# Splitting the first four token loads of a fused transformer block over two issuing engines

## Chip, cores and metric

The kernel runs on one core of a Trainium2 chip. The metric is device time in microseconds for one execution of the whole block, the median of several runs. The profile is of one further execution.

## What is computed

A pre-norm block over 2048 tokens of width 640 with 32 heads of 20: layer norm, query, key and value projections, attention in four segments of 512 tokens with a compressive memory carried from segment to segment, output projection and residual; then a second layer norm, a two-layer feed-forward net of width 1728 with SiLU, and a residual.

```python
x = A_x
h = x + _A_ref(_layernorm(x), A_wq, A_wk, A_wv, A_wo, A_beta)   # attention with memory, 4 segments
h2 = h + _B_ref(_layernorm(h), B_w1, B_w2)                      # silu(x @ w1) @ w2
...
# _A_ref, per segment s:
logits = jnp.einsum('bhqd,bhkd->bhqk', qs, ks) * scale + mask
p = _softmax(logits, axis=-1)
a_dot = jnp.einsum('bhqk,bhkd->bhqd', p, vs)
...
o = g * a_mem + (1.0 - g) * a_dot
M = M + jnp.einsum('bhld,bhle->bhde', phi(ks), vs)
```

All inputs and the output are bf16.

## The kernel before

The tokens are 16 blocks of 128. Segment s holds the blocks 4s to 4s+3. Each segment has a front (layer norm, transposes, projections), ticks (scores, exponentials and weighted sums, one head group of four at a time), a memory update and a back (output projection, second layer norm, feed-forward). Work of neighbouring segments overlaps.

Everything is declared as tasks with the tiles that they read and write. The order of the tasks is a written list, `ORDER` (line 362): every engine carries out its own tasks in the order of that list, and one tracker derives the semaphore waits from the tiles. A name such as `x1:1` means task x1 with buffer 1; a suffix such as `/S` or `/A` chooses the engine where a task allows several. An engine never overtakes: an instruction that waits holds up all behind it on the same engine.

The list begins with these rows:

```python
halfc:0 mt2 mta2 x0:0 mt3 iota sel mt1 zpad x1:1 x2:2 vpad0 mta3 n1_st0:0 epsc x3:3 mt0 warm:0 n1_rs0 w_q:0 n1_st1:6
n1_rs1 n1_st2:2 n1_rs2 n1_st3:3 n1_rs3 n1_ap1:0 mtb3 re_wq2/G:0 w_k fill20:0 fill9:0 re_wk3/G:0 n1_tp1:2 n1_te1/A:1 n1_ap0:1
```

The tasks around the change are these.

- x0 to x3 (line 579) load the token blocks 0 to 3 into `x_tok`, 160 KB each, one transfer a block. w_q, w_k and w_wv (line 582) load the query, key and value weights, 800 KB each, the first two into space that is later `sT`. beta (line 591) loads the 32 gates, repeated over the partitions. All are issued by SyncE (SP) in the order of the list: x0, x1, x2, x3, wq, wk, wv, beta. The later loads, of which the second token group (blocks 4 to 7) and then wo come first, wait until the first fifth of the key weights is repacked.
- n1_st (lines 721 and 724, VectorE) takes the statistics of a block, two halves and their aggregate; n1_rs (lines 730 and 732, GpSimd) adds epsilon and raises to the power -0.5; n1_ap (line 738, VectorE) normalises into a buffer of `xn_rot`. VectorE's order is the statistics of the blocks 0, 1, 2, 3 and then the normalisation of the blocks 1, 0, 2, 3. Block 1 and block 3 share buffer 0 of `xn_rot`, so the normalisation of block 3 waits until block 1 has been transposed.
- n1_tp (line 747, TensorE) transposes a block by five matmuls against an identity, in the order 1, 0, 2, 3; n1_te (lines 756 on ScalarE and 757 on VectorE) writes the result to `tT`, the blocks 1, 0 and 3 on ScalarE and block 2 on VectorE.
- re_wq and re_wk (lines 694 and 696; VectorE, ScalarE and GpSimd) repack the query and key weights by head into `wqr` and `wkr`, in five parts each.
- pr (lines 546 and 547, TensorE) are the projections, qe (lines 831 and 832) their evictions. The first projection needs all four blocks in `tT` and one part of `wqr`.
- fill20 and fill9 (line 616, TensorE) are 29 matmuls of the zero tile `zpad`, which stand in TensorE's order ahead of the first transpose. warm (line 597, ScalarE) is one activation on the same tile, ahead of all other work of ScalarE, with the load of the function table before it. ScalarE issues no transfer in this kernel.

The lines that declare the loads:

```python
def dma(name, reads, writes, fn, prio, bw, kind="plain", lane=None, engs=(SP,)):
    ln = T.lane(name) if lane is None else lane
    ...
def load_x(b0, n, prio, bw=2.1, kind="plain", engs=(SP, AC)):
    s0 = b0 % 12
    dma(f"x{b0}", [(W["wk"], [0])] if b0 >= 4 else [], [(X[b], [0]) for b in range(b0, b0 + n)],
        lambda e: e.dma_start(out=x_tok[:, s0:s0 + n, :], in_=xv[:, b0:b0 + n, :]), prio, bw, kind, engs=engs)
```

A lane is a semaphore of its own, so each load can be waited for by itself. Where `engs` holds one engine and the list names none, the task goes to that one.

Of the kernel before, what the change touches and what calls it, by code (L numbers as in the profile page):

```python
# [11 lines left out]
PE, AC, DV, PO, SP = "pe", "act", "dve", "pool", "sp"  # L12
# [453 lines left out]
def build(nc, es, A_x, A_wq, A_wk, A_wv, A_wo, A_beta, B_x, B_w1, B_w2, out):  # L466
# [89 lines left out]
    def dma(name, reads, writes, fn, prio, bw, kind="plain", lane=None, engs=(SP,)):  # L556
        ln = T.lane(name) if lane is None else lane

        def emit(eng):
            T.add(eng, lambda e: fn(e), reads=R(*reads), writes=R(*writes), lane=ln)  # L560
        cost = {"tr": 1.31, "plain": 0.47, "sb": 0.72, "fix": 0.47}[kind]
        t = G.task(name, {e: cost for e in engs}, emit, reads, writes, prio, mode=kind, bw=bw)
        return t
# [12 lines left out]
# [5 lines that stand above are left out]
    def load_w(k, dst, src, prio, bw, wr, kind="plain", engs=(SP, AC)):  # L581
        dma("w_" + k, [(W["wk"], [0])] if kind == "plain" else [], wr, lambda e: e.dma_start(out=dst, in_=src), prio, bw, kind, engs=engs)

    cw = lambda w: w.rearrange("(c p) e -> p c e", p=128)
    load_x(0, 1, -100, 2.30, "fix", (SP,))
    load_x(1, 1, -99, 2.33, "fix", (SP,))
    load_w("wv", wv_sb[:, :, :], cw(A_wv), -98, 4.96, [(W["wv"], [0])], "fix", (SP,))
    load_x(2, 1, -97, 4.79, "fix", (SP,))
    load_x(3, 1, -96, 4.82, "fix", (SP,))
    dma("beta", [], [(C, ["beta_bc"])],  # L590
        lambda e: e.dma_start(out=beta_bc[:, :],
                              in_=A_beta.rearrange("(o n) -> o n", o=1).to_broadcast([128, H])), -92, 4.65, "fix")
# [642 lines left out]
def bass_sequential_preLN__memory_aug_infini_attn__dense_activation_silu__prompt_kernel(  # L1235
    nc, A_x, A_wq, A_wk, A_wv, A_wo, A_beta, B_x, B_w1, B_w2, out
):
    es = ExitStack()
    with es:
        T, finals, _ = build(nc, es, A_x, A_wq, A_wk, A_wv, A_wo, A_beta, B_x, B_w1, B_w2, out)  # L1240
        with nc.Block() as block:
            T.emit(nc, block, es, final_waits=finals)
# [28 lines left out]
```

## Time and profile before

| | |
|---|---|
| median of 3 runs | 300.82 us (300.63 to 301.13) |
| profiled execution | 301.27 us |
| its span, first to last instruction | 299.5 us |
| TensorE, matmuls | 281.5 us busy, 94% |
| VectorE | 223.3 us, 75% |
| ScalarE | 211.5 us, 71% |
| GpSimd | 146.5 us, 49% |
| transfers | 24.79 MB, mean 83 GB/s |
| granted TensorE clock | full in every slice |

The span is shorter than the execution's time by what lies before its first and after its last instruction. Matmuls are pipelined, so TensorE's busy share isn't its share of peak. SPq is the issuing of transfers by SyncE: its rows show how long an issue takes, not the transfer; the time to landing is counted from the start of the issue to the last of the semaphore's updates. DVE is VectorE, ACT ScalarE, POOL GpSimd, PE TensorE and PEld its weight loads.

### The profile page before, as it was taken

What the parts mean: (1) busy time and instruction counts of PE and PEld (TensorE: products, weight loads), DVE (VectorE), ACT (ScalarE), POOL (GpSimd) and SP (SyncE); (2) the same over time, 40 slices, a digit from 0 to 9 for tenths busy, and PEclk for the clock granted to TensorE, in tenths of its full rate; (3) what the DMA queues carried; (4) which work ended last, traced back from release to release, by engine and by line L of the source; (5) the groups of instructions that cost most, each with busy time, mean ns of one, the idle gap of its engine ahead of it and who ended that gap; (6) DMA issues with size and microseconds to landing.
All of it is one profiled execution on the core that took longest, in us unless ns stands there. A gap on an engine that the chain in (4) does not pass through costs nothing.

```text
span 299.5 us, 9583 instructions
## 1 busy us (share of the span) xinstructions
PE 281.5 (94%) x4069; PEld 158.7 (53%) x4096; DVE 223.3 (75%) x455; ACT 211.5 (71%) x271; POOL 146.5 (49%) x294
## 2 busy tenths in 40 slices
PE   6899789979979999998999999999999999999996
PEld 4553345536634444565654554666654556764574
DVE  6699999788997777779878967497764875727622
ACT  3598999999889999965789858868888651004500
POOL 5767487664945735634743852555854420300000
PEclk9999999999999999999999999999999999999999
DMA  7766937965644410164438521601130032333001
GB/s 208 258 187 141 163 50 174 180 144 103 120 91 37 134 21 2 24 85 92 81 93 126 48 44 24 96 14 33 22 66 2 2 40 51 81 74 109 3 22 66
DMA packets 48586, 24.79 MB, mean 83 GB/s; under 512 B 38880, under 2 KB 47456, under 8 KB 48544
## 3 DMA queue, kind: packets, MB, share of 16 engines
q1 hardware_dynamic: 48544, 24.19, 39.0%
q8 instruction: 32, 0.52, 0.7%
q14 instruction: 10, 0.08, 0.1%
HBM read 10.41 MB, written 2.62 MB: 44 GB/s over the span
## 4 chain that ended last, share of the span: by engine, by line
PE 72%; DVE 11%; ACT 9%; DMA 4%; issue 2%; SPq 1%; POOL 0%; ACTq 0%; DVEq 0%; POOLq 0%
PE ps_all L546 38%; PE ps_all L547 17%; ACT PT L914 8%; PE ps_all L901 6%; PE ps_all L949 4%; PE ps_all L616 2%; PE ps_all L978 2%; DMA tT<-otok 1%; DMA tT<-xn_rot 1%; DMA phiKt<-phiK 1%; PE ps_all L982 1%; DVE on L1015 1%; DVE QK L832 1%; DVE phiQ L851 1%; DVE xn_rot L738 1%
## 5 line engine op out<-in xcount | busy, mean ns | idle before, releaser
L914 ACT ACTIVATE PT<-ps_all 128x1024 bf16<-128x1024 f32 x160 | 154.8, 1027 | 22.3 <-PE ps_all L901 21.3
L926 POOL TENSOR_SCALAR_AFFINE_SELECT PT<-PT 128x512 bf16<-128x512 bf16 x128 | 81.9, 646 | 59.6 <-ACT PT L914 56.2
L1160 ACT ACTIVATE th<-ps_all 128x512 f32<-128x512 f32 (+1 forms) x56 | 31.7, 586 | 32.5 <-PE ps_all L546 25.7
L546 PE MATMUL ps_all<-w_sb,sT 128*128 128x320 bf16 x360 | 52.1, 300 | 0.0
L1166 DVE SCALAR_TENSOR_TENSOR sT<-th,ps_all 128x512 bf16<-128x512 f32 (+1 forms) x56 | 36.3, 663 | 20.5 <-ACT th L1160 20.1
L546 PEld LDWEIGHTS ps_all<-w_sb,sT 128*128 128x128 bf16 x360 | 34.3, 98 | 14.8 <-issue 1.5
L546 PE MATMUL ps_all<-tT,w_sb 128*128 128x512 bf16 x161 | 37.5, 379 | 1.0 <-DVE sT L1166 0.3
L721 DVE BATCH_NORM_STATS2 stt<-x_tok 128x6 f32<-128x320 bf16 x64 | 27.8, 476 | 1.1 <-DMA x_tok<-in_A_x_dram 1.0
L1023 POOL TENSOR_TENSOR otok<-on 128x320 bf16<-128x320 bf16 x24 | 19.4, 812 | 15.4 <-DVE on L1015 12.3
L546 PEld LDWEIGHTS ps_all<-tT,w_sb 128*128 128x128 bf16 x172 | 15.9, 98 | 18.2 <-DVE sT L1166 1.1
L1202 DVE SCALAR_TENSOR_TENSOR x_tok<-ps_all,x_tok 128x640 bf16<-128x640 f32 (+1 forms) x17 | 13.2, 780 | 14.6 <-PE ps_all L546 14.4
L949 PE MATMUL ps_all<-PT,Vx 128*32 128x384 bf16 (+3 forms) x512 | 22.9, 301 | 0.7 <-DVE w_sb L832 0.7
L964 DVE TENSOR_SCALAR oTs<-ps_all,lsc 128x512 bf16<-128x512 f32 x28 | 20.8, 744 | 3.7 <-PE ps_all L949 3.6
L547 PE MATMUL ps_all<-tT,w_sb 128*32 128x512 bf16 x352 | 22.4, 380 | 0.0
L730 POOL TENSOR_TENSOR rst<-mvt,eps_c 128x1 f32<-128x1 f32 x32 | 6.8, 214 | 30.0 <-DVE mvt L724 30.0
L1015 DVE TENSOR_TENSOR on<-ps_all,rd 128x640 bf16<-128x640 f32 x24 | 19.8, 824 | 0.8
L832 DVE CAST QK<-ps_all 128x512 bf16<-128x512 f32 x25 | 17.0, 683 | 4.1 <-PE ps_all L546 2.6
L732 POOL TENSOR_TENSOR rst<-rst,eps_c 128x1 f32<-128x1 f32 x32 | 18.3, 571 | 2.5
L738 DVE TENSOR_SCALAR xn_rot<-x_tok,mvt,rst 128x640 bf16<-128x640 bf16 x32 | 16.6, 534 | 2.9 <-POOL rst L732 1.9
L546 PE MATMUL ps_all<-wv_sb,tT 128*128 128x320 bf16 x120 | 18.3, 300 | 0.3 <-ACT PT L914 0.2
L949 PEld LDWEIGHTS ps_all<-PT,Vx 128*32 128x32 bf16 x512 | 12.0, 96 | 10.8 <-issue 2.6
L901 PE MATMUL ps_all<-QK 20*128 20x512 bf16 (+3 forms) x240 | 15.1, 301 | 2.6 <-DVE QK L832 1.2
(91 smaller groups left out, 389.9 us busy)
## 6 DMA issues: line engine op xcount, KB each, us to landing
out_dram<-x_tok SPq DMA_DIRECT2D x15, 160.0 KB, 1.9
w_sb<-in_B_w_dram SPq DMA_DIRECT2D x5, 432.0 KB, 4.6
x_tok<-in_A_x_dram SPq DMA_DIRECT2D x3, 640.0 KB, 6.1
w_sb<-in_B_w_dram SPq DMA_DIRECT2D x3, 480.0 KB, 5.1
QKV<-QK SPq DMA_DIRECT2D x12, 72.0 KB
sT<-in_A_wq_dram SPq DMA_DIRECT2D x1, 800.0 KB, 6.6
sT<-in_A_wk_dram SPq DMA_DIRECT2D x1, 800.0 KB, 8.3
wv_sb<-in_A_wv_dram SPq DMA_DIRECT2D x1, 800.0 KB, 9.8
```

What stands on the lines that cost most here:

```text
L546: return [lambda e: e.matmul(out, lhsT=lhsT, rhs=rhs, start=start, stop=stop)]
L547: return [lambda e, p=p: e.matmul(out[p:p + 32, :], lhsT=lhsT[:, p:p + 32], rhs=rhs, start=start, stop=stop, tile_position=(0, p)) for p i ...
L721: T.add(DV, lambda e, hh=hh: e.bn_stats(out=stt[:, s, 6 * hh:6 * hh + 6], in_=xb[:, 320 * hh:320 * hh + 320]), reads=R((xa, xsub)), writes ...
L832: (lambda e: e.tensor_copy(out=o, in_=i_))
L901: fns.append(lambda e, j=j, o=o, r=r, q0=q0, q1=q1, qa=qa, ka=ka: e.matmul(ps_all[:, o:o + q1 - q0], lhsT=ka[32 * r:32 * r + DH, 128 * j:1 ...
L914: T.add(AC, lambda e: e.activation(out=pt[:, pta.slot, q0:q0 + 2, 0:width], in_=sc3[:, b0:b0 + 2, 0:width], func=ACT.Exp, scale=SCALE), re ...
L926: fns.append(lambda e, v=v: e.affine_select(out=v, in_=v, pattern=[[0, 4], [1, 128]], compare_op=ALU.is_ge, fill=0.0, base=0, channel_mult ...
L949: fns.append(lambda e, j=j, r=r, h=h, pa=pa, pt=pt, co=co, q0=q0, ji=ji: e.matmul(bank(po)[32 * r:32 * r + 32, q0:hi], lhsT=Vx[:, vx.slot, ...
L964: f = lambda e: e.tensor_scalar(out=o, in0=i_, scalar1=lsc[:, g:g + 1], scalar2=None, op0=ALU.mult)
L1015: T.add(DV, lambda e: e.tensor_tensor(out=on[:, ona.slot, :, :].rearrange("p b (x e) -> p b x e", e=DH), in0=v[:, :, :, 0:DH], in1=r2.unsq ...
L1160: T.add(AC, lambda e: e.activation(out=th[:, tha.slot, lo:hi], in_=bank(ps)[:, lo:hi], func=ACT.Tanh, scale=0.5), reads=R((ps, [0])), writ ...
L1166: T.add(DV, lambda e: e.scalar_tensor_tensor(out=sT[:, f, lo:hi], in0=th[:, tha.slot, lo:hi], scalar=1.0, in1=bank(ps)[:, lo:hi], op0=ALU. ...
```

## The change

x1 and x3 are given to ScalarE. Since the list puts both ahead of warm, they are ScalarE's first two instructions, ahead of its table load. SyncE issues x0, x2, wq, wk, wv, beta. The list is the same, and the orders of TensorE, VectorE and GpSimd stay as they are. The transfers are the same in shape, size and number.

```diff
     load_x(0, 1, -100, 2.30, "fix", (SP,))
-    load_x(1, 1, -99, 2.33, "fix", (SP,))
+    load_x(1, 1, -99, 2.33, "fix", (AC,))
     load_w("wv", wv_sb[:, :, :], cw(A_wv), -98, 4.96, [(W["wv"], [0])], "fix", (SP,))
     load_x(2, 1, -97, 4.79, "fix", (SP,))
-    load_x(3, 1, -96, 4.82, "fix", (SP,))
+    load_x(3, 1, -96, 4.82, "fix", (AC,))
```

The numbers in these calls are hints of a planner that made the list; with the list written out they have no effect.

## The prediction

> **What bounds the kernel now.** I read the page first, then the chain that ended last, the waits and the timeline of the first 25 us, and the single issues of the token loads.
>
> ```profile
> span 299.5 us, 9583 instructions
> PE 281.5 (94%) x4069; PEld 158.7 (53%) x4096; DVE 223.3 (75%) x455; ACT 211.5 (71%) x271; POOL 146.5 (49%) x294
> PE 72%; DVE 11%; ACT 9%; DMA 4%; issue 2%; SPq 1%; POOL 0%; ACTq 0%; DVEq 0%; POOLq 0%
> ```
>
> TensorE is busy 94% of the span and carries 72% of the chain; transfers carry 4%. The change touches only the first issues, so the question is what starts TensorE's real work. The chain answers in order of time (start, duration, what):
>
> ```profile
> 2.66 5.83 PE ps_all L616 x29
> 8.49 0.29 PE ps_all L747 x5
> ...
> 8.81 1.90 ACT tT L756 x3
> ...
> 10.76 4.50 PE ps_all L547 x80
> ...
> 20.65 2.16 PE ps_all L546 x15
> ...
> 22.83 0.83 DVE Vx L799
> ```
>
> The 29 filler matmuls (L616) multiply a zero tile. They start when VectorE has written that tile and run to 8.49 in TensorE's fixed order, ahead of the first transpose (L747). No token block is in this chain before 8.49. Then come five matmuls that transpose block 1, three ScalarE evictions and the first projection at 10.76; TensorE and then VectorE carry on from there without a transfer. So an earlier token block brings nothing unless the fillers were waiting for it, and they do not; a later one costs once it has used up the slack of the layer norm that runs beside the fillers.
>
> The timeline of that layer norm (start, busy, engine, in brackets the idle time before and what ended it):
>
> ```profile
> 3.12 0.89 DVE L721 BATCH_NORM_STATS2 stt<-x_tok 128x6 f32<-128x320 bf16 x2 [0.52 <-DMA x_tok<-in_A_x_dram]
> ...
> 5.41 0.89 DVE L721 BATCH_NORM_STATS2 stt<-x_tok 128x6 f32<-128x320 bf16 x2 [0.17 <-DMA x_tok<-in_A_x_dram]
> ...
> 6.46 0.83 DVE L721 BATCH_NORM_STATS2 stt<-x_tok 128x6 f32<-128x320 bf16 x2
> ...
> 7.45 1.11 DVE L738 TENSOR_SCALAR xn_rot<-x_tok,mvt,rst 128x640 bf16<-128x640 bf16 x3
> ...
> 7.97 0.64 POOL L732 TENSOR_TENSOR rst<-rst,eps_c 128x1 f32<-128x1 f32 x1
> ...
> 8.92 0.45 DVE L738 TENSOR_SCALAR xn_rot<-x_tok,mvt,rst 128x640 bf16<-128x640 bf16 x1 [0.36 <-POOL mt L659]
> ```
>
> VectorE takes the blocks 0, 1, 2, 3. It waits 0.52 us for x0 and 0.17 us for x2; x1 and x3 are there in time. The fourth normalisation, at 8.92, writes buffer 0 of xn_rot, whose last reader is the transpose of block 1. That ends at 8.49 + 0.29 = 8.78, while GpSimd's power for block 3 ends at 7.97 + 0.64 = 8.61. The view names GpSimd's next instruction, but that one isn't needed; by the code it is TensorE's transpose. So GpSimd is 0.17 us early, and the statistics of block 3 may come 0.17 us later for nothing. The three other normalisations are done by 7.45 + 1.11 = 8.56, also ahead of 8.78.
>
> **The change part by part.** The issues of the load queue before:
>
> ```profile
> 0.81 1.83 SPq L579 DMA_DIRECT2D x_tok<-in_A_x_dram  x4
> 2.68 0.43 SPq L582 DMA_DIRECT2D sT<-in_A_wq_dram  x1
> 3.16 0.53 SPq L582 DMA_DIRECT2D sT<-in_A_wk_dram  x1
> 3.73 0.56 SPq L582 DMA_DIRECT2D wv_sb<-in_A_wv_dram  x1
> 4.33 1.60 SPq L591 DMA_DIRECT2D beta_bc<-in_A_beta_dram  x1
> ```
>
> The four token issues run from 0.81 to the next issue at 2.68: 1.87 / 4 = 0.47 us each. Two leave the queue, so x2 is issued at 1.28 and not 1.75, and wq, wk, wv and beta each 2 x 0.47 = 0.94 us earlier (wq at 1.74).
>
> ScalarE gets two issues ahead of its table load:
>
> ```profile
> 0.80 1.28 ACT L597 ACT_TABLE_LOAD   x1 [0.80 <-PEq L1256]
> 2.64 1.27 ACT L597 ACTIVATE w_sb<-zpad 128x1280 bf16<-128x1280 bf16 x1 [0.55 <-DVE zpad L595]
> 8.81 1.90 ACT L756 ACTIVATE tT<-ps_all 128x640 bf16<-128x640 f32 x3 [4.90 <-PE ps_all L747]
> ```
>
> No ScalarE issue is in this trace. By the SP rows both take 0.94 us: x1 goes out at about 0.80 and x3 at 1.27, which is 0.48 and 0.95 us earlier than before, and the table load moves to 1.74. The warm-up activation ends at 2.64 + 1.27 = 3.91 before and by about 4.4 after (1.74 + 1.28 + 1.27 = 4.29). ScalarE then has nothing until 8.81, after 4.90 us of idle time, so this costs nothing; even two issues at the 1.60 us of beta's row would end the warm-up by 6.6.
>
> When the blocks land. One answer for each of the four issues, x0 to x3 (duration of the issue in ns, its start, and the time to landing):
>
> ```profile
> L579 SPq DMA_DIRECT2D x_tok<-in_A_x_dram x1: 408/408/408, 0.8 to 0.8; - x1
> ...
> DMA to landing us min/median/max: 2.3/2.3/2.3
> ```
>
> ```profile
> L579 SPq DMA_DIRECT2D x_tok<-in_A_x_dram x1: 417/417/417, 1.3 to 1.3; - x1
> ...
> DMA to landing us min/median/max: 2.3/2.3/2.3
> ```
>
> ```profile
> L579 SPq DMA_DIRECT2D x_tok<-in_A_x_dram x1: 432/432/432, 1.7 to 1.7; - x1
> ...
> DMA to landing us min/median/max: 3.7/3.7/3.7
> ```
>
> ```profile
> L579 SPq DMA_DIRECT2D x_tok<-in_A_x_dram x1: 432/432/432, 2.2 to 2.2; - x1
> ...
> DMA to landing us min/median/max: 4.0/4.0/4.0
> ```
>
> So x0 lands at 0.8 + 2.3 = 3.1, x1 at 1.28 + 2.3 = 3.6, x2 at 1.7 + 3.7 = 5.4, and x3 at 2.2 + 4.0 = 6.2 for a use at 6.46. After the change x3 goes out 0.95 us sooner and needn't be late. x2 lands no later than its 5.4 unless the whole stream is slower. What can become later is x0, since x1 now goes out beside it instead of 0.47 us behind it. Its tolerance: the 0.17 us for which VectorE waits for x2 vanishes if x2 is in time, and 0.17 us are spare at GpSimd. Together 0.34 us, so x0 may land at 3.44 for nothing. To price a shared start I take the stream's rates by the microsecond (the last column is GB/s; 1 GB/s is 1 KB in a us):
>
> ```profile
> 1.00:2.00 1.00, 0.00 (x0) 0.00 (x0) 0.28 (x1) 1.00 (x1) 0.93 (x7) 1.00 0.17 15
> 2.00:3.00 1.00, 0.34 (x2) 0.28 (x3) 0.60 (x2) 0.45 (x2) 0.71 (x5) 1.00 0.87 287
> 3.00:4.00 1.00, 1.00 (x7) 0.69 (x5) 0.88 (x2) 0.91 (x1) 0.00 (x0) 1.00 1.01 178
> ```
>
> By 3.0 there are 15 + 287 = 302 KB through, and the 320 KB of x0 and x1 by 3.0 + 18/178 = 3.1. If the two share the stream evenly, x0 is through only then instead of at 2.0 + 145/287 = 2.5, 0.6 us later, less what lies between the last bytes and the landing, which was 3.1 - 2.5 = 0.6 us for x0 and 3.6 - 3.1 = 0.5 us for x1. So x0 lands at 3.1 + 0.5 = 3.6, and TensorE's first projection moves by 3.6 - 3.44 = 0.16 us. The lower end is x0 landing at 3.1 as before: 0.00. A gain is excluded here, since the fillers end at 8.49 either way. I take the middle, +0.1 us.
>
> [...] No run here shows two queues yet.
>
> The weights. They land up to 0.94 us earlier. Who waits for them:
>
> ```profile
> POOL wkr L696 <- DMA sT<-in_A_wk_dram: 1.4, 1, 1.4
> ...
> DVE wkr L696 <- DMA sT<-in_A_wk_dram: 1.0, 1, 1.0
> ...
> POOL wqr L696 <- DMA sT<-in_A_wq_dram: 0.5, 1, 0.5
> ```
>
> These waits are real, but behind them VectorE and ScalarE wait again, for TensorE:
>
> ```profile
> 12.50 0.69 DVE L832 CAST w_sb<-ps_all 128x512 bf16<-128x512 f32 x1 [0.27 <-PE ps_all L547]
> ...
> 12.71 2.05 PEld L547 LDWEIGHTS ps_all<-tT,wkr 128*32 128x32 bf16 x40
> ...
> 13.15 0.60 ACT L831 ACTIVATE w_sb<-ps_all 128x512 bf16<-128x512 f32 x1 [0.80 <-PE ps_all L547]
> ```
>
> TensorE is the chain from 10.76 to 22.8 but for short gaps and takes the key weights at 12.71 with no wait. So earlier weights lengthen those waits by what they shorten the first: 0.00. The next loads on SP (the second token group and wo) wait for the key weights' repacking and move earlier too, with nothing behind them that the chain names. If the cover were gone, all 0.94 us could show; that is the lower end.
>
> Sum: 0.00 (ScalarE) + 0.1 (x0) + 0.00 (weights) = +0.1 us. The profiled execution took 301.27 us, 1.8 more than its span; the median of the three runs is 300.82. The same step on the median gives 300.9 us. About 0.2%, 0.6 us, is what a measurement of this kernel can tell from no change.
>
> **The rivals.**
>
> *x0 lands much later.* The stream falls from 287 to 178 GB/s between 3 and 4 us, just after the weights are issued (2.68 to 4.33). If their issuing makes that dip, it moves 0.94 us earlier, onto x0 and x1. Then by 3.0 only 15 + 178 = 193 KB are through, the 320 KB at 3.0 + 127/178 = 3.7, x0 lands at 4.2, and 4.2 - 3.44 = 0.76 us go through the statistics, the normalisations and the transposes to the first projection: 301.6 us. It decides from a landing after 3.44 and shows as slower from 4.04. For it: the dip stands right behind these issues, and x2 and x3, which lie in it, took 3.7 and 4.0 us against 2.3. Against it: x0 and x1 are issued ahead of the weights on their queues, and the trace does not show that the weights' issues cause the dip.
>
> *The earlier weights carry through.* If VectorE's and GpSimd's repacking, 0.94 us ahead, shortens what follows after 22.8, where the chain goes over to VectorE, the time falls by up to 0.94 us: 299.9. Against it: every chain piece from 10.76 to 22.8 is TensorE's.
>
> *The second queue doesn't start when ScalarE does.* If ScalarE's issues land 1 us later than I assume, x1 (needed when x0's statistics are done, at 3.12 + 0.89 = 4.01 at the earliest) and x3 (needed at 6.46) land at 0.80 + 1 + 2.3 = 4.1 and at most 1.27 + 1 + 4.0 = 6.3; the statistics slip by 0.1 us, inside the 0.34 us: 300.8.
>
> **How the numbers follow.** Forecast 0.5, the late queue 0.06: both within 0.2%. x0 much later 0.27. Weights carry through 0.17, which takes in that the first 10 us, with other phases between the engines, come out better for a reason that I don't see. The forecast alone spans 300.5 to 301.3 (the step's two ends and the spread of the three runs, 300.63 to 301.13). The range goes down to 300.0, nearly all of the weights' gain, and up to 301.9, the late x0 at 301.6 and the same spread above it. Faster 0.17, same 0.56, slower 0.27.
>
> **What would show it.** In the profile after: the fillers still 2.66 to 8.49; the first projection at 10.76 to 10.9; x0's first statistics between 3.1 and 3.6 and no wait for x2; two issues on ScalarE ahead of the table load; wq issued near 1.74 and the waits for wk shorter by up to 0.94 us, with the waits of L831 and L832 for TensorE longer. Wrong would be a first projection after 11.3, a filler that starts later, or an equal first projection with another end, which would put the cause behind 10.76.

## The result and the profile after

The changed kernel takes 301.85 us (median of 22 runs, 300.60 to 304.51) against 300.77 us of the kernel before on the same chip (22 runs, 299.15 to 303.14): a ratio of 1.004, 95% interval 1.0025 to 1.0054, which is 0.8 to 1.6 us. The forecast was no change that can be measured, at 300.9 us; it is slower. A few executions of several kernels, at a granted clock of 0.989 to 0.994, are 2 to 4 us longer than the others; such an execution counts in the ratios below where it is less than 1.5% above the fastest of its kernel.

The profiled execution of the changed kernel took 301.62 us with a span of 299.9 us. Outside the span lie 1.7 us, against 1.8 us before, so the loss is inside it. The lines of its page:

```profile
span 299.9 us, 9610 instructions
PE 283.8 (95%) x4096; PEld 158.1 (53%) x4096; DVE 224.1 (75%) x455; ACT 211.3 (70%) x271; POOL 146.7 (49%) x294
q10 hardware_dynamic: 288, 0.33, 0.4%
q14 instruction: 10, 0.08, 0.1%
PE 71%; ACT 14%; DVE 9%; DMA 2%; issue 1%; POOL 1%; SPq 0%; ACTq 0%
```

The queue rows give packets, MB and share. The new queue q10 carries ScalarE's two blocks. ScalarE's share of the chain rises from 9% to 14%. The timeline of the start (start, busy, engine, in brackets the idle time before and what ended it):

```profile
0.80 0.88 ACTq L579 DMA_DIRECT2D x_tok<-in_A_x_dram  x2
0.81 0.90 SPq L579 DMA_DIRECT2D x_tok<-in_A_x_dram  x2
1.72 1.28 ACT L597 ACT_TABLE_LOAD   x1 [1.72 <-PEq L1256]
1.75 0.44 SPq L582 DMA_DIRECT2D sT<-in_A_wq_dram  x1
2.66 4.82 PE L616 MATMUL ps_all<-zpad 128*128 128x256 bf16 x29 [2.66 <-DVE zpad L595]
3.01 1.27 ACT L597 ACTIVATE w_sb<-zpad 128x1280 bf16<-128x1280 bf16 x1
3.87 0.89 DVE L721 BATCH_NORM_STATS2 stt<-x_tok 128x6 f32<-128x320 bf16 x2 [1.27 <-DMA x_tok<-in_A_x_dram]
...
4.92 0.83 DVE L721 BATCH_NORM_STATS2 stt<-x_tok 128x6 f32<-128x320 bf16 x2
...
7.89 2.04 DVE L738 TENSOR_SCALAR xn_rot<-x_tok,mvt,rst 128x640 bf16<-128x640 bf16 x4
...
12.99 0.69 DVE L832 CAST w_sb<-ps_all 128x512 bf16<-128x512 f32 x1 [0.98 <-PE ps_all L547]
...
13.63 0.60 ACT L831 ACTIVATE w_sb<-ps_all 128x512 bf16<-128x512 f32 x1 [1.01 <-PE ps_all L547]
```

Both queues start at 0.8 us. x0, the one block that was needed first, comes 0.75 us later: the first statistics start at 3.87 instead of 3.12. The three blocks behind it are then in time. The fillers, which the prediction had ending at 8.49 "either way", end at 2.66 + 4.82 = 7.48. The chain that ended last up to the first projection (start, duration, what):

```profile
0.81 3.04 DMA x_tok<-in_A_x_dram
...
8.35 0.82 PE ps_all L747 x10
9.17 0.78 DVE xn_rot L738
9.95 0.05 issue
9.99 0.47 PE ps_all L747 x5
10.46 0.02 issue
10.48 0.71 ACT tT L756
11.20 0.04 issue
11.24 1.90 PE ps_all L547 x29
```

x0 lands at 0.81 + 3.04 = 3.85 and now heads the chain, with no filler in it. The fourth normalisation takes 0.78 us where it took 0.45, and the first projection starts at 11.24 instead of 10.76.

That is 0.48 us at the start. A second loss lies far from the edit. ScalarE's timeline at 52 to 56 us and at 160 to 162 us, first of the kernel before, then of the changed one:

```profile
52.66 3.95 ACT L914 ACTIVATE PT<-ps_all 128x1024 bf16<-128x1024 f32 x4
...
160.97 0.60 ACT L1160 ACTIVATE th<-ps_all 128x512 f32<-128x512 f32 x1 [0.16 <-PE ps_all L546]
```

```profile
52.18 2.85 ACT L914 ACTIVATE PT<-ps_all 128x1024 bf16<-128x1024 f32 x3
55.40 1.02 ACT L914 ACTIVATE PT<-ps_all 128x1024 bf16<-128x1024 f32 x1 [0.37 <-PE ps_all L901]
...
161.32 0.60 ACT L1160 ACTIVATE th<-ps_all 128x512 f32<-128x512 f32 x1 [0.43 <-PE ps_all L901]
```

Four exponentials ran back to back before; now there is a hole of 0.37 us ahead of the fourth. At the same place of the feed-forward the idle time goes from 0.16 to 0.43 us. What TensorE makes of the second hole, before and after:

```profile
166.52 0.28 PE L1063 MATMUL ps_all<-Vx,phiKt 128*32 128x42 bf16 x16
166.93 0.40 PE L901 MATMUL ps_all<-QKV 20*128 20x256 bf16 x8
```

```profile
166.59 0.28 PE L1063 MATMUL ps_all<-Vx,phiKt 128*32 128x42 bf16 x16
167.27 0.40 PE L901 MATMUL ps_all<-QKV 20*128 20x256 bf16 x8 [0.40 <-ACT PT L914]
```

The step from one to the other is 0.41 us before and 0.68 us after, so this hole passes to TensorE in full (+0.27). Of the first hole, ScalarE's start is 0.30 us later and 0.18 us are won back at the sixth exponential behind it, which waits 0.18 us less; 0.12 to 0.13 us reach TensorE. Together 0.4 us where they arise.

What is left of all this at the end can be read off TensorE's 4096 weight loads, which have the same order in both kernels, by setting each against its counterpart in the trace of before. The changed kernel's are 0.49 us late at 20 us, 0.56 at 60 us, only 0.07 at 150 us, 0.34 from 169 us on and 0.36 at the end. So in this pair of traces the second hole is most of the difference of the spans (299.9 against 299.5), and the late start is mostly lost again by 150 us.

### The profile page after: what moved, and what is told of

It is laid out like the page before. It is cut to its first block, busy times and chain, and to the rows that moved or that the text cites. A ratio compares the mean times of both kernels' runs of the same rounds, so it can differ in the third digit from the quotient of the medians.

```text
span 299.9 us, 9610 instructions
## 1 busy us (share of the span) xinstructions
PE 283.8 (95%) x4096; PEld 158.1 (53%) x4096; DVE 224.1 (75%) x455; ACT 211.3 (70%) x271; POOL 146.7 (49%) x294
## 4 chain that ended last, share of the span: by engine, by line
PE 71%; ACT 14%; DVE 9%; DMA 2%; issue 1%; POOL 1%; SPq 0%; ACTq 0%
PE ps_all L546 40%; PE ps_all L547 17%; ACT PT L914 12%; PE ps_all L901 6%; PE ps_all L949 4%; PE ps_all L978 2%; DVE stt L721 2%; ACT th L1160 1%; PE ps_all L982 1%; DMA tT<-otok 1%; DMA x_tok<-in_A_x_dram 1%; DVE xn_rot L738 1%; DVE on L1015 1%; DVE QK L832 1%; DVE w_sb L832 1%
## 5 line engine op out<-in xcount | busy, mean ns | idle before, releaser
L546 PE MATMUL ps_all<-tT,w_sb 128*128 128x512 bf16 x172 | 39.8, 379 | 0.4 <-DVE rd L1009 0.3
L832 DVE CAST QK<-ps_all 128x512 bf16<-128x512 f32 x25 | 17.0, 683 | 4.1 <-PE ps_all L546 2.6
```

The lines of the kernel that those rows point to most:

```text
L546: return [lambda e: e.matmul(out, lhsT=lhsT, rhs=rhs, start=start, stop=stop)]
L832: (lambda e: e.tensor_copy(out=o, in_=i_))
```

## The experiments

Each row is one kernel; the ratio is to the kernel before on the same chip, with its 95% interval. "More" is the number of instructions that ScalarE has more than in the kernel before. The two holes are the idle times of ScalarE at the places above; a dash means none shown, or the 0.15 to 0.16 us of the kernel before.

| kernel | ratio | more | holes | fillers end | first statistics | first projection | span |
|---|---|---|---|---|---|---|---|
| before | 1 | 0 | - | 8.49 | 3.12 | 10.76 | 299.5 |
| before, once more | one execution, 300.48 us | 0 | - | 8.07 | 3.11 | 11.13 | 298.8 |
| changed | 1.0040 (1.0025 to 1.0054) | 2 | 0.37, 0.43 | 7.48 | 3.87 | 11.24 | 299.9 |
| changed, once more | 1.0040 (1.0022 to 1.0058) | 2 | 0.38, 0.43 | 7.83 | 3.82 | 11.19 | 300.6 |
| weights held | 1.0051 (1.0029 to 1.0073) | 2 | 0.38, 0.43 | 8.52 | 3.89 | 11.26 | 300.5 |
| x1 later | 1.0114 (1.0071 to 1.0156) | 2 | 0.37, 0.43 | 7.94 | 3.17 | 11.20 | 299.9 |
| both held | 1.0029 (1.0007 to 1.0050) | 2 | 0.38, 0.43 | 8.13 | 3.18 | 10.39 | 299.4 |
| copy held | 1.0042 (1.0014 to 1.0071) | 2 | 0.37, 0.43 | 8.10 | 3.80 | 10.84 | 300.5 |
| before, two activations more | 1.0009 (0.9986 to 1.0031) | 2 | 0.36, 0.43 | 8.55 | 3.18 | 10.81 | 299.4 |
| order swapped | 1.0015 (0.9995 to 1.0036) | 0 | - | 7.41 | 3.61 | 10.64 | 298.8 |
| 24 fillers | 1.0003 (0.9978 to 1.0028) | 0 | - | 7.41 | 3.19 | 10.90 | 299.3 |
| x1 alone | 0.9995 (0.9976 to 1.0014) | 1 | - | 7.42 | 3.92 | 11.20 | 299.3 |
| changed, one activation more | 1.0022 (1.0002 to 1.0043) | 3 | - | 7.86 | 3.86 | 10.89 | 300.6 |
| both held, one activation more | 1.0015 (0.9990 to 1.0041) | 3 | - | 7.71 | 3.05 | 10.75 | 299.4 |

**Why x0 is late: the shared start or the weights.** The first experiment keeps both queues and holds back the query weights, and with them all behind them, until the zero tile is written, so that they are issued as late as in the kernel before. The second keeps the early weights and holds back x1 until a mask is written.

```diff
-            T.add(eng, lambda e: fn(e), reads=R(*reads), writes=R(*writes), lane=ln)
+            T.add(eng, lambda e: fn(e), reads=R(*reads) + (C.keys(["zpad"]) if name == "w_q" else []), writes=R(*writes), lane=ln)
```

> The changed kernel, but SyncE issues the query weights (and all behind them) only when the zero tile is written, at about 2.65 us as before the change instead of 1.75; x1 and x3 stay on ScalarE. Theory A, x0 shares the stream with x1 from its first packets: x0 still lands at 3.6 to 3.9 us, the first statistics start then and the time is 0.7 to 1.2 us over the kernel before. Theory B, the earlier issue of the weights slows the stream under x0: x0 lands by 3.3 us and the time is within 0.3 us of the kernel before.

The second has `C.keys(["mt2"]) if name == "x1"` in that place.

> The changed kernel, but ScalarE issues x1 only after one of GpSimd's first masks, at about 1.5 us instead of 0.80, and x3 behind it; SyncE as in the change, with the weights early. Theory A (shared start): x0 lands at 3.1 to 3.3 us and the time is within 0.3 us of the kernel before, or up to 0.3 us below it since VectorE no longer waits for x2. Theory B (early weights): x0 lands after 3.5 us and the time is 0.7 us or more over the kernel before.

The timeline with the weights held (issue of wq, the first statistics):

```profile
2.63 0.39 SPq L582 DMA_DIRECT2D sT<-in_A_wq_dram  x1
...
3.89 0.89 DVE L721 BATCH_NORM_STATS2 stt<-x_tok 128x6 f32<-128x320 bf16 x2 [1.29 <-DMA x_tok<-in_A_x_dram]
```

wq goes out at 2.63, and x0 is as late as in the changed kernel (3.89 against 3.87). So the weights are not what delays x0. With x1 at 1.42 instead of 0.80, x0 is back:

```profile
3.17 0.89 DVE L721 BATCH_NORM_STATS2 stt<-x_tok 128x6 f32<-128x320 bf16 x2 [0.57 <-DMA x_tok<-in_A_x_dram]
4.45 0.89 DVE L721 BATCH_NORM_STATS2 stt<-x_tok 128x6 f32<-128x320 bf16 x2 [0.15 <-DMA x_tok<-in_A_x_dram]
...
6.81 0.89 DVE L721 BATCH_NORM_STATS2 stt<-x_tok 128x6 f32<-128x320 bf16 x2 [0.24 <-DMA x_tok<-in_A_x_dram]
```

It is the shared start. In this kernel it is x1 and x3 that come late, behind the early weights, and the first projection is as late as in the changed kernel (11.20). Its ratio of 1.0114 rests on six executions, of which four took 301.61 to 302.78 us and two 305.42 and 305.61, so its size means little. But the middle of the four, 302.3, is still 1.7 us over the 300.60 of the kernel before on that chip, more than any step of its trace explains; this stays open.

**Is a late x0 dear in itself? And the fillers?** The kernel before with x1 ahead of x0 in the list, all on SyncE; and the kernel before with 24 fillers instead of 29.

```diff
-halfc:0 mt2 mta2 x0:0 mt3 iota sel mt1 zpad x1:1 x2:2 vpad0 mta3 n1_st0:0 epsc x3:3 mt0 warm:0 n1_rs0 w_q:0 n1_st1:6
+halfc:0 mt2 mta2 x1:1 mt3 iota sel mt1 zpad x0:0 x2:2 vpad0 mta3 n1_st0:0 epsc x3:3 mt0 warm:0 n1_rs0 w_q:0 n1_st1:6
```

> The kernel before, all loads on SyncE, with x1 issued first and x0 second; VectorE still takes x0 first. x0 then lands at 3.5 to 3.6 us instead of 3.1. If the landing of x0 sets the start of TensorE's work in the mean run, the first statistics start at 3.6, 0.45 us late, of which 0.17 us are made up at x2: 0.3 us over the kernel before. If the fillers set it, as the prediction had it: 0.1 us. If the landing of x0 doesn't matter: 0.0.

```diff
-n1_rs1 n1_st2:2 n1_rs2 n1_st3:3 n1_rs3 n1_ap1:0 mtb3 re_wq2/G:0 w_k fill20:0 fill9:0 re_wk3/G:0 n1_tp1:2 n1_te1/A:1 n1_ap0:1
+n1_rs1 n1_st2:2 n1_rs2 n1_st3:3 n1_rs3 n1_ap1:0 mtb3 re_wq2/G:0 w_k fill20:0 fill4:0 re_wk3/G:0 n1_tp1:2 n1_te1/A:1 n1_ap0:1
```

> The kernel before with 24 filler matmuls instead of 29. At 213 ns each they end by 7.8 us at the latest, ahead of the first normalised block at 7.85. If the fillers bind in the mean run, as the prediction had it, the first projection comes up to 0.35 us earlier and the time is 0.3 us lower. If the fillers mostly end before the layer norm, since their spacing falls from 213 to 109 ns at a time that differs from run to run (7.75 us in the profile of before, 5.79 in that of after): within 0.2 us, and the first transpose waits for VectorE.

TensorE's timeline, first with the order swapped (29 fillers), then with 24:

```profile
2.66 4.75 PE L616 MATMUL ps_all<-zpad 128*128 128x256 bf16 x29 [2.66 <-DVE zpad L595]
8.09 1.76 PE L747 MATMUL ps_all<-ident,xn_rot 128*128 128x128 bf16 x20 [0.67 <-DVE xn_rot L738]
10.64 2.34 PE L547 MATMUL ps_all<-tT,wqr 128*32 128x512 bf16 x40 [0.79 <-ACT tT L756]
```

```profile
2.66 4.75 PE L616 MATMUL ps_all<-zpad 128*128 128x256 bf16 x24 [2.66 <-DVE zpad L595]
7.66 1.76 PE L747 MATMUL ps_all<-ident,xn_rot 128*128 128x128 bf16 x20 [0.25 <-DVE xn_rot L738]
10.90 2.34 PE L547 MATMUL ps_all<-tT,wqr 128*32 128x512 bf16 x40 [1.48 <-POOL wqr L696]
```

29 fillers took as long here as 24 there. With the order swapped, x0 is 0.5 us late, the fillers end early, and the first projection is earlier than in the kernel before. With 24 fillers the projection waits for GpSimd's repacking of the query weights. Neither time can be told from the kernel before. So the fillers bind in some executions, as in the trace of before, and not in others.

**The stretched normalisation.** In the changed kernel the fourth normalisation runs beside GpSimd's repacking of the query weights, which begins at 9.24, and takes 0.78 us. This kernel is the changed one with the three GpSimd repackings moved behind that normalisation in the list and the first of them waiting for it. The wait (the edit of the list is left out):

```diff
-                T.run(eng, fns, R(*rr), R(*ww))
+                T.run(eng, fns, R(*rr) + ([("xn", 0, 0)] if (k, c) == ("wq", 2) else []), R(*ww))
```

> The changed kernel, but GpSimd's first copy of the query weights waits until VectorE has normalised block 3. In the profile of the changed kernel that normalisation took 0.79 us beside this copy, and 0.45 us in the profile of before, where the copy had hardly begun. If the copy stretches it: 0.45 us again, the first projection near 10.9 us instead of 11.24, the time 0.3 us under the changed kernel and still 0.4 to 0.8 us over the kernel before. If the stretch has another cause: 0.79 us still, and the time of the changed kernel.

The four normalisations take 1.70 us together instead of 2.04, and the first projection starts at 10.84. So the overlap does stretch it, by 0.34 us. But the time stays where it was, at 1.0042. The next kernel holds back both, x1 until the mask and wq until the zero tile, and the kernel before was profiled once more, unchanged.

```diff
-            T.add(eng, lambda e: fn(e), reads=R(*reads), writes=R(*writes), lane=ln)
+            T.add(eng, lambda e: fn(e), reads=R(*reads) + (C.keys([{"w_q": "zpad", "x1": "mt2"}[name]]) if name in ("w_q", "x1") else []), writes=R(*writes), lane=ln)
```

> Both holds together: ScalarE issues x1 at about 1.4 us and x3 behind it, SyncE the weights at about 2.65 us. Theory (a load issued beside x0 delays x0, and weights issued ahead of x3 delay x3): x0 lands at 3.1 to 3.2 us, x3 by 5.5 us, VectorE waits for no block after x0, the first projection starts at 10.3 to 10.7 us unless the fillers end late, and the time is between 0.3 us under and 0.2 us over the kernel before. If the second queue costs by itself: 0.5 us or more over.

> The kernel before, unchanged, for another draw of the time at which the matmul spacing falls from 213 to 109 ns. If that time is free of the kernel, the 29 fillers end elsewhere than at 8.49 us, and where they end by 7.9 us the first projection starts at 10.3 to 10.6 us, set by VectorE, instead of 10.76. If the 8.49 us is fixed for this kernel: 8.4 to 8.6 again.

TensorE's timeline of the kernel with both held, and the chain of the kernel before in its second trace:

```profile
2.66 5.47 PE L616 MATMUL ps_all<-zpad 128*128 128x256 bf16 x29 [2.66 <-DVE zpad L595]
...
10.39 2.34 PE L547 MATMUL ps_all<-tT,wqr 128*32 128x512 bf16 x40 [0.88 <-ACT tT L756]
```

```profile
2.68 7.33 DMA sT<-in_A_wq_dram
10.01 0.05 issue
10.07 0.93 POOL wqr L696 x2
11.00 0.14 issue
11.13 1.89 PE ps_all L547 x29
```

These two turn the question round. With both held the first projection is the earliest of all, 10.39, and the kernel is still slower than the one before, by 0.2 to 1.5 us where at most 0.2 was expected. The kernel before, in another execution, starts it at 11.13, as late as the changed one, because wq landed at 10.01 instead of 9.26; that execution is among the shortest (298.8 us). The start cannot be the whole cause.

**One issue alone.** The changed kernel with x3 back on SyncE.

```diff
-    load_x(3, 1, -96, 4.82, "fix", (AC,))
+    load_x(3, 1, -96, 4.82, "fix", (SP,))
```

> Half of the change: x1 on ScalarE at 0.80 us, x3 stays on SyncE behind x2, so the weights go out 0.47 us earlier and not 0.94. Theory A (shared start): x0 lands at 3.6 to 3.9 us, the first projection starts near 11.2 us and the time is 0.7 to 1.2 us over the kernel before, all of the change's loss. If the loss needs both loads on ScalarE: x0 lands by 3.4 us and the time is within 0.4 us.

```profile
3.92 0.89 DVE L721 BATCH_NORM_STATS2 stt<-x_tok 128x6 f32<-128x320 bf16 x2 [1.31 <-DMA x_tok<-in_A_x_dram]
```

x0 is as late as in the changed kernel, the first projection is at 11.20, and there is no loss: 0.9995 (0.9976 to 1.0014). So a late x0 alone doesn't cost the 0.7 to 1.2 us of theory A. What the changed kernel has and this one has not, beside x3 on ScalarE, are ScalarE's two holes.

**The holes: a matter of ScalarE's count.** All kernels so far with two more instructions on ScalarE had the holes, at the same instructions; those with none or one had not. The next three change the count by nothing but very small activations: the warm-up activation is split into a long one and one or two of one column a half.

```diff
-    G.task("warm", {AC: 1.15}, lambda e_: T.add(AC, lambda e: e.activation(
-        out=w2_sb[:, NF - 1:NF + 1, :], in_=zpad[:, 0:1].unsqueeze(2).to_broadcast([128, 2, D]), func=ACT.Tanh),
+    G.task("warm", {AC: 1.15}, lambda e_: T.run(AC, [(lambda e, lo=lo, hi=hi: e.activation(out=w2_sb[:, NF - 1:NF + 1, lo:hi], in_=zpad[:, 0:1].unsqueeze(2).to_broadcast([128, 2, hi - lo]), func=ACT.Tanh))
+        for lo, hi in [(0, D - 2)] + [(D - 2 + i, D - 2 + i + 1) for i in range(2)]],
```

This is for the kernel before with two more; the changed kernel and the one with both held get one more (`D - 1`, `range(1)`). The changed kernel itself ran beside them.

> The kernel before, all loads on SyncE, with two further one-column activations on ScalarE behind the warm-up, long before its next work. Theory P (place of ScalarE's instructions): two more instructions at ScalarE's start, of whatever kind, move a fetch of its instructions behind a wait, so ScalarE stalls 0.3 us near 55 us and 0.3 us near 161 us as in the changed kernel; x0 lands at 3.1 us and the first projection is as before; the time is 0.4 to 0.9 us over the kernel before. Theory A alone (only x0's landing costs): no stall there and within 0.2 us.

> The changed kernel with one further one-column activation on ScalarE behind the warm-up, so three more instructions than before instead of two. Theory P: the fetch then falls ahead of the wait and is hidden behind running work, the stalls near 55 and 161 us are gone, and of the changed kernel's 1.1 us only the late start is left: 0.0 to 0.5 us over the kernel before. Theory A alone: as the changed kernel, 0.8 to 1.3 us over.

> Both holds (x1 on ScalarE at 1.4 us, weights at 2.65 us) and one further activation on ScalarE. Theory P with theory A: x0 at 3.1 us, no stalls near 55 and 161 us, first projection at 10.3 to 11 us: 0.4 us under to 0.2 us over the kernel before, and 0.4 us or more under the run with both holds alone. If the second queue costs by itself: still 0.6 us or more over.

> The changed kernel unchanged, beside the three others on the same chip: 0.75 to 1.6 us over the kernel before, with the stalls near 55 and 161 us, x0 at 3.6 to 3.9 us and the fillers ending elsewhere than at 7.48 us.

ScalarE in the kernel before with two activations more, and in the changed kernel with one more:

```profile
54.79 1.94 ACT L914 ACTIVATE PT<-ps_all 128x1024 bf16<-128x1024 f32 x2 [0.36 <-PE ps_all L901]
...
160.83 0.60 ACT L1160 ACTIVATE th<-ps_all 128x512 f32<-128x512 f32 x1 [0.43 <-PE ps_all L901]
```

```profile
52.17 3.93 ACT L914 ACTIVATE PT<-ps_all 128x1024 bf16<-128x1024 f32 x4
...
162.07 0.60 ACT L1160 ACTIVATE th<-ps_all 128x512 f32<-128x512 f32 x1 [0.15 <-PE ps_all L546]
```

The holes come with two activations and without any second queue, and they go from the changed kernel with one instruction more. That is shown, and the traces show which instructions are struck; that a fetch of instructions is behind it, as theory P has it, is the author's conjecture and not shown. Numbering ScalarE's recorded instructions from 0 (waits and issues counted), the holes of the kernels with two more lie at the numbers 63, 191 and 319, the third at about 282 us. Each is an activation that starts 0.32 to 0.36 us after the wait before it; elsewhere in these traces an activation that comes directly behind a wait, with ScalarE idle, starts some 0.04 us after it. The kernel before has one such hole too, ahead of ScalarE's last activation, which is its number 319:

```profile
282.22 0.38 ACT L1160 ACTIVATE th<-ps_all 128x256 f32<-128x256 f32 x1 [0.28 <-ACT th L1160]
```

The same activation has no idle time before it in the kernel with x1 alone, where it is number 320. So the change adds two holes, and the place in the count decides, not the activation.

In the traces the cost of the second hole is plain. TensorE's weight loads lose 0.27 to 0.28 us between 165 and 169 us in all seven kernels with two more instructions, at most 0.01 us in the six others with 29 fillers, and from there to the end no kernel gains or loses more than 0.03 us. The first hole costs them 0.11 to 0.14 us at 57 us, but what comes between 60 and 150 us hides whether it lasts. In the times the cost is shown less sharply. Beside each other on one chip the changed kernel has 1.0040 and the one without holes 1.0022, a difference of 0.0018 or 0.5 us, close to the 0.4 us that TensorE loses in the trace; both held with and without the holes, on two chips, differ by 0.0014. But the intervals overlap, and the kernel before with two activations more, at 1.0009 (0.9986 to 1.0031), can be told neither from no loss nor from one of 0.4 us.

## Why the prediction was wrong, point by point

**"The fillers end at 8.49 either way" failed.** This was the step that made the start insensitive. The same 29 matmuls end between 7.41 and 8.55 in the thirteen traces that have 29, and this does not follow the edits: 8.49 and 8.07 in the kernel before, 7.48 and 7.83 in the changed one. In the single rows the matmuls follow each other at 213 ns at first and at 109 ns later; the switch came at 7.75 us in the first trace of the kernel before, at 5.79 in that of the changed one, and between 5.62 and 7.95 over all traces, 3.0 to 5.3 us after the first filler. The profile's granted clock reads 1.00 throughout. What makes the spacing fall, and what sets the moment, is not shown; the two ends of the kernel before alone lie 0.42 us apart. The one trace at hand had the third-latest end of the thirteen, and the prediction took it for a constant. Nor were the fillers the only thing that could bind: in the second trace of the kernel before the first projection waited for wq.

**The landing of x0 was put too early.** Even sharing, which no run had shown, gave 3.6, the range 3.1 to 3.6; it landed at 3.85, and between 3.80 and 3.92 started the first statistics in every kernel with both queues from 0.8 us. The stream after (the last column is GB/s):

```profile
2.00:3.00 1.00, 0.34 (x2) 0.28 (x3) 0.60 (x2) 1.00 (x1) 0.71 (x5) 1.00 0.83 243
3.00:4.00 1.00, 1.00 (x7) 0.69 (x6) 0.14 (x1) 0.99 (x1) 0.00 (x0) 1.00 1.05 346
```

Between 2 and 3 us it moves 243 KB instead of 287. By the records of single packets, x0's data starts moving at 2.15 and its last packet starts at 3.30 (1.85 and 2.60 before), beside x1's from 1.84 to 3.05; x3's begin at 3.05 behind x1's, and x2's at 3.32 behind x0's. x3 isn't needed for the delay, since with x3 on SyncE the first statistics start at 3.92. Between 2.15 and 3.05 there start 92 packets of x0 and 101 of x1, of 1280 bytes each. So the direction and about the even sharing held, and the landing was put 0.25 us too early. With the prediction's own tolerance of 3.44, x0 at 3.85 gives +0.41 us, and the first projection moved by 0.48; that these are close is chance. Where the fourth normalisation isn't stretched, x0's data is used at 3.80 and 3.86 and the first projection is 0.08 and 0.13 us later than in the trace of before (copy held; changed, one activation more; with x1 alone it waits for wq's repacking instead). That is about the forecast +0.1, and the stretch makes the rest.

**The rival "x0 lands much later" had a value near the result and the wrong mechanism.** It gave 301.6 us by the weights' issuing; with the weights held until 2.63, x0 was no earlier. That 301.85 lies within the stated range, which goes up to 301.9 for this rival's sake, is therefore luck.

**"Weights 0.00" held, and the weights' repacking met a neighbour.** wq went out at 1.75 (forecast 1.74), and the waits of L832 and L831 for TensorE grew from 0.27 to 0.98 and from 0.80 to 1.01, as said. But GpSimd's repacking of wq, from 9.24 (9.31 before), fell beside the fourth normalisation, which now starts at 9.15 instead of 8.92, and stretched it by 0.34 us, most of the 0.48 us at the start. It is the late x0 that brings the two together: with the weights held until 2.63 the repacking starts at 9.27, and the four normalisations take 2.04 us all the same. The prediction had no term for this.

**"ScalarE 0.00" was right at the start and wrong 50 us on.** The issues took 0.88 us together (0.94 forecast), the table load moved to 1.72 (1.74), the warm-up ended at 4.28 (4.29). Its "idle until 8.81" was no answer to what two more instructions do to those behind them: they cost TensorE 0.13 us at 57 us and 0.27 us at 167 us. The trace of before had a single row of the kind, the 0.28 us ahead of ScalarE's last activation, and no rival had it.

**The second queue** began at 0.80, not late.

**A sign of being wrong named in "What would show it"**, another end without a later first projection, which puts the cause behind 10.76, was seen in the kernel with both held: the first projection comes earlier than before, and the kernel is slower.

The account in total: the step that failed for certain is "this costs nothing" for ScalarE's two further instructions. It measured 0.27 us at the end of every trace with two more, and 0.13 us where the first hole arises. The other is the fixed start: the first projection is 0.06 to 0.48 us later in the changed kernel than in the two traces of before. But the start doesn't decide the end. Over the thirteen traces TensorE is between 0.78 us ahead of the trace of before and 1.10 us behind it at 150 us, and this doesn't follow the first projection: the second trace of the kernel before starts 0.38 us late and is 0.78 ahead at 150 us, and the changed kernel with one activation more starts 0.13 late and is 1.10 behind. So 0.27 of the measured 0.8 to 1.6 us is shown; what the first hole and the late start leave at the end, and where the rest of the loss comes from, is open. One thing that blurs it: TensorE's waits for the transposed attention output at about 130 and 137 us are 0.42 and 0.77 us in the kernel before, 0.98 and 0.82 us in the changed kernel with one activation more, 0.99 and 0.16 us in the kernel with both held; they move an execution's end by some 0.6 us with no pattern that these runs reveal. No variant was faster than the kernel before.

## What to carry to other kernels

A load moved to a second queue at the same instant shared the stream with the load that is needed first, and delayed it (first statistics at 3.87 instead of 3.12 us); starting the second queue 0.6 us later gave x0 its old landing here, but no gain in time. Do not read a bound off filler matmuls in one trace: their end moved by up to 1.1 us between executions here, whatever the edit. When an edit adds or removes instructions at the head of an engine's list, compare that engine's idle times all the way through, and pad the list by one small instruction to tell the edit's own effect from that of the shifted places.

## What the runs showed of the hardware that was not expected

- ScalarE's recorded instructions number 63, 191 and 319 are 128 apart. In the kernels with two more instructions each of them is an activation directly behind a wait on a semaphore, and each has a hole. With none, 63 and 191 come behind running work and show no hole, and 319 comes behind a wait and shows one. With one or three more no such activation stands at these numbers, and no hole shows. What makes the step of 128 is not shown. The q14 row of the profile's page, of the kind "instruction", has 10 packets with 0.08 MB, 8 KB a packet; in the changed kernel packets of that queue start at 56.06, 162.85 and 282.64 us, 0.6 to 1.6 us after the three holes end, and in the kernel before, which has only the third hole, at 56.06, 162.91 and 282.87.
- Issuing two token loads took ScalarE about as long as SyncE: 0.88 us against 0.90 in the changed kernel.
- A normalisation on VectorE of 0.45 us took 0.78 us beside a copy on GpSimd, and the four took 1.70 us again instead of 2.04 with the copy held back.
